# One cast and one subtraction for three split blocks, and another order in the last batch: a masked attention with a rational feed-forward layer

## The chip, the cores and the metric

The kernel runs on one core of a Trainium2 chip. A core has TensorE (PE, with weight loads listed apart as PEld), VectorE (DVE), ScalarE (ACT), GpSimd (POOL) and SyncE (SP), and DMA queues that SP, POOL and ACT issue into. The metric is the device time in microseconds (us) of one execution; the time before is the median of three runs. A separate profiled execution gives the trace.

## The reference

Inputs: q, k, v of 8 batches x 8 heads x 576 rows x 64; a number tau; w_in (512 x 2048), w_out (2048 x 512), and the coefficients a (4) and b (2).

```
scores = q @ k.T / 8
scores = where(scores >= max(scores) - tau, scores, -1e9)
attn   = softmax(scores)            # each row apart
x      = (attn @ v) laid out as 4608 tokens x 512
h      = x @ w_in
P      = a0 + a1 h + a2 h^2 + a3 h^3
Q      = 1 + |b0| |h| + |b1| h^2
out    = (P / (Q + 1e-6)) @ w_out
```

All inputs and the output are float32.

## The kernel before

**Attention units.** Two heads (a pair) are worked on at once; there are 4 pairs in a batch and 32 in all. The 576 rows of a pair make four full units of 128 rows and one short unit of 64 rows (number 4, the "rest"). A unit is: scores on TensorE into three PSUM banks (f_qk, L805 to L816), row maxima on VectorE (L822), threshold and mask on ScalarE (L829, L837), exponential with row sum on ScalarE (L841), reciprocal on VectorE (L852), the normalised weights split into a high and a low float16 half (L859 through the helper at L326 or L328, and L863), and two DMA transposes into a pT tile (L873). Two units of a pair share one pT tile (there are two), and then come three products with V on TensorE (f_av, L934), whose result is split into two float16 halves of x (L944, L950). The first batch takes another way through float32 transposes on TensorE (L886, L917).

**V.** V of a pair is loaded whole into one of NV tiles (L691, L695, L719), its largest magnitude is taken (L704 or L706), and when all four pairs of a batch have theirs, scale_ops (L412 to L445) makes one scale for the batch. After that each V is split into halves in place (L746 to L753, seen as L326, L328, L750, L320). A V tile is free again when the third product with it is done.

**Visits.** A batch is walked through in two visits of each pair: `half` (units 0 and 1), and later `other + rest` (units 2, 3 and the short one); the last pair takes all at once, and the second visits run backwards. K and Q are loaded at each visit (load_ops).

**Feed-forward chunks.** 256 tokens make a chunk: ("m", batch, 0) from units 0 and 1, ("m", batch, 1) from units 2 and 3, and the short rows of four batches make ("r", 0, 0) and ("r", 1, 0). Each chunk runs through four groups of four blocks of 128 hidden units (moe_ops). A group is: 48 float16 matmuls with w_in (L1051), the result to SBUF on ScalarE (L1060), the absolute value (L1065 or L1067), the rational function as a row of operations on 1024 columns (L1071 to L1093, of which L1078 and L1081 on ScalarE), and then the product with w_out. Of the four blocks, the first goes into that product as float32 (L1114); the other three (in_parts, PARTS = 3) are split into two parts of the type that TensorE multiplies faster: a cast (f_gh, seen as L318 on ScalarE or L320 on VectorE) and a subtraction (f_gl, L1101), each on 256 columns, into a g tile; then three matmuls for each half of the tokens (L1110). There are two g tiles. The last group of all is cut into two of two blocks. When a chunk's four groups are done, the sum is scaled (L1124, L1119) and stored (L1133 for an "m" chunk, one store a tile of 128 tokens; L1137 for an "r" chunk, two stores a tile).

**Weights.** w_in and w_out arrive as 64-bit numbers and are decoded on ScalarE and VectorE in the first part of the run, at times set by WHEN.

**Order.** Nothing is scheduled at run time. The program makes a list of operations, each with an engine (or two to choose from, FLEX) and a duration, a key, what it comes after and which buffers it takes (Hold) and drops. Plan.order walks through them in its own model of time: it starts on each engine the operation that can start first, and among those within TOL of it the one with the lowest key. Where two engines can do an operation, `sooner` weighs them with a price for each engine (START, EARLY and PRICE, by time). What comes out is one fixed order on each engine. Keys of attention units are their positions; a group of the feed-forward layer has the key max(previous + SPACING, last unit of its chunk + LEAD), those of the last batch end + ENDK + ENDS x i. LAST names the order of the last three chunks: ("m", 7, 0), ("m", 7, 1), ("r", 1, 0). A buffer that is not free holds up the engine that comes to the operation, and all behind it on that engine; so does a V load that waits on POOL's queue.

Of the kernel before, what the change touches and what calls it, by code (L numbers as in the profile page):

```python
# [8 lines left out]
F32 = mybir.dt.float32  # L9
F32R = mybir.dt.float32r  # L10
F16 = mybir.dt.float16
# [4 lines left out]
ALU = mybir.AluOpType  # L16
# [7 lines left out]

POOLS = {"e": 3, "hi": 2, "pT": 2, "st": 8, "sc": 2, "t": 8, "u": 3, "g": 2, "x": 3, "xr": 1}

B2, B3, BA, B1, BH = [(0, 1, 2), (3, 4, 5)], [(0, 1, 2)], [(3,), (4,), (5,)], [(7,), (6,), (5,)], [(5,), (6,)]


LEAD, SPACE0, SPACING = 4.776489494, 2.7365, 2.085146464
ENDK, ENDS = 4.7452, 10.130284218

WHEN = [(-4.7413, 1.6268), (5.5534, 0.8332), (13.0267, 0.2709), (15.0744, 0.5122)]

V0, V1 = -3.870384768, -4.680004432

SINGLE = 21

VISITED = 8

FIRST = [(0, 0, 8), (1, 0, 16), (0, 8, 16)]
LAST = (0, 1, 2)
SOON = 1

NQ = 2

NV = 5

EARLY_BP = 8

# [4 lines left out]
PARTS = 3  # L57
# [2 lines left out]

ALL = 2.0 ** 100

PLAIN = (0, 1, 2, 3, 4)

UP = 2.0 ** -14
TPD = 1.3
# [11 lines left out]
        "ev": {"ACT": 0.465, "DVE": 0.6}, "ev1": {"ACT": 0.156, "DVE": 0.196}, "A": {"ACT": 0.583, "DVE": 0.341},  # L78
        "gh": {"ACT": 0.31, "DVE": 0.2}, "wh": {"ACT": 0.57, "DVE": 0.38}, "vc": {"ACT": 0.7, "DVE": 0.25}, "twice": {"ACT": 0.2, "DVE": 0.13}}

START = {"ACT": 2.958800008, "DVE": 3.4788}
START_END = 61.53014116
EARLY = {"ACT": 2.0183, "DVE": 2.9268}
EARLY_END = 1205.239479456
PRICE = {"ACT": 0.7389, "DVE": 2.6699}

TOL = {"PE": 0.098890645, "ACT": 0.1137, "DVE": 0.0398, "POOL": 0.1, "DMA": 0, "GD": 0}
WARM, WARM_END = 0.6, 400.0

LOADS_END = 120.0  # L90

LATE = 2.0

SPARE = {'t': 2, 'u': 1, 'g': 1, 'sc': 1}

# [24 lines left out]
class Plan:  # L120
# [21 lines left out]
    def op(self, eng, dur, key, fn, after=(), take=(), drop=()):  # L142
        engs = {eng: dur} if isinstance(eng, str) else eng
        o = Op(engs, key, fn, [x for x in after if x is not None], list(take), list(drop))
        o.rank, o.tiling = self.rank, "ff"
        self.ops.append(o)
        return o
# [10 lines left out]
    def sooner(self, e, t, o, free, can):  # L158
        price = START if t < START_END else EARLY if t < EARLY_END else PRICE
        for x, dur in o.engs.items():  # L160
            if x != e:
                begin = max(free[x], o.ready[x])
                begin += sum(p.engs[x] for p in can[x] if p.key < o.key and len(p.engs) == 1 and p.ready[x] <= begin)
                if begin + dur * price[x] < t + o.engs[e] * price[e]:
                    return True
        return False

    def order(self):
# [6 lines left out]
        free = dict.fromkeys(engines, 0.0)  # L175
        tiling = "f"
# [13 lines left out]
        while left:  # L190
            best = None
            for e in engines:
                starts = []
                for o in can[e]:
                    t = max(free[e], o.ready[e])
                    for h in o.take:
                        spot = None if h.pool in line and line[h.pool][-1] is not h and len(self.pools.get(h.pool, ())) <= SPARE.get(h.pool, 99) else self.spot(h, t)
                        if spot is None:
                            t = None
                            break  # L200
                        t = max(t, spot[0])
                    if t is not None:
                        if e == "PE":
                            t = max(t, free[e] + TURN.get((tiling, o.tiling[0]), 0.0))
                        starts.append((t, o))
                if not starts:
                    continue
                first = min(t for t, _ in starts)
                starts = sorted([x for x in starts if x[0] <= first + TOL[e]] if all(len(o.engs) == 1 for _, o in starts)
                                else starts, key=lambda x: (x[1].key, x[1].n))  # L210

                keep = [(t, o) for t, o in starts if len(o.engs) == 1 or not self.sooner(e, t, o, free, can)]
                if not keep:
                    continue
                first = min(t for t, _ in keep)
                t, o = min(((t, o) for t, o in keep if t <= first + TOL[e]), key=lambda x: (x[1].key, x[1].n))
                if best is None or t < best[0]:
                    best = (t, o, e)
            assert best is not None, "no op can start"
            t, o, e = best  # L220
# [3 lines left out]
            if e == "PE" and self.warm is not None and t < WARM_END:  # L224
                n = int((t - free[e]) * WARM / 0.22)
# [10 lines left out]
            if e == "PE":  # L236
                tiling = o.tiling[1]
# [34 lines left out]
def fr(ap):  # L272
    return ap.bitcast(F32R)
# [3 lines left out]
def masked_attention_rational_ffn(  # L277
# [12 lines left out]
    nc = tc.nc  # L290
    B, NP, D, S = qT.shape
    S = S // 2
    DM, DFF = w_in.shape
    P = 128
    NT = S // P
    REM = S - NT * P
    NF = DFF // P
    NFP = NF // 2
    NC = DM // P
    CT = 256  # L300
# [4 lines left out]
    op = plan.op  # L305
# [10 lines left out]
    def copy(dst, src):  # L316
        if plan.eng == "ACT":
            nc.scalar.copy(dst, src)  # L318
        elif plan.eng == "DVE":
            nc.vector.tensor_copy(dst, src)  # L320
        else:
            nc.gpsimd.tensor_scalar(dst, src, 1.0, 1.0, ALU.mult, ALU.mult)
# [9 lines left out]
    def tensor_tensor(dst, x, y, how):  # L332
# [5 lines left out]

    forms = {"t": ([P, 4 * CT], F32), "u": ([P, DM], F32), "e": ([P, 2 * S], F32), "hi": ([P, 2 * S], F16),
             "pT": ([P, 2, 2, 2 * NT + 1, P], F16), "st": ([P, 8], F32), "sc": ([P, 4], F32),  # L340
             "g": ([P, 2, CT], F32), "x": ([P, 2, NP, CT], F16), "xr": ([P, 2, NP, CT], F16)}
    places = {x: [const.tile(f, d, name=f"{x}{i}") for i in range(POOLS[x])] for x, (f, d) in forms.items()}

    def place(h):
        return places[h.pool][h.slot]
# [181 lines left out]
    for i in range(NW):  # L527
        pieces = []
        for c in range(NC):
            n = i * NC + c  # L530
# [6 lines left out]
            key = w_key(i, c)  # L537

            o6, box = decode_ops(n, key, load, hold)
# [9 lines left out]
        key = w_key(i, NC)  # L549
# [17 lines left out]
    wo_done = []  # L567

    def in_parts(f):
        return f % NC >= NC - PARTS  # L570

    for f in range(NF):
# [6 lines left out]
        key = w_key(f // NC, NC + f % NC)  # L579
# [5 lines left out]
        o, box = decode_ops(NC * NW + f, key, load, hold)  # L585
# [15 lines left out]
    visits = []  # L601
    for bb in range(B):
        v0 = bb * NP
        if bb < VISITED:
            visits += [(v0 + i, half) for i in range(NP - 1)] + [(v0 + NP - 1, half + other + rest)]
            visits += [(v0 + i, other + rest) for i in range(NP - 2, -1, -1)]
        else:
            visits += [(v0 + i, half + other + rest) for i in range(NP)]
# [60 lines left out]

    def is_plain(bp, t):  # L670

        return bp < NP and t in PLAIN

    v_ops = {}

# [343 lines left out]
    def moe_ops(ck, f0, nb, p, begins, ends, soon):  # L1019
# [18 lines left out]
        def on(e, d, *rest):  # L1038
            return op(e, size(e, d), *rest)
# [52 lines left out]
        def f_g():  # L1092
            nc.vector.scalar_tensor_tensor(box["r"], box["r"], a0, box["q"], ALU.add, ALU.mult)  # L1093

        def f_gh(j):
            box["g", j] = place(hg[j])
            copy(fr(box["g", j][:, 0]), box["r"][:, j * CT:(j + 1) * CT])

        def f_gl(j):
            g = box["g", j]  # L1100
            nc.vector.tensor_tensor(fr(g[:, 1]), box["r"][:, j * CT:(j + 1) * CT], g[:, 0], ALU.subtract)  # L1101

        def f_g2(j, tt):
            f = f0 + j
            if begins and j == 0:
                acc[tt] = bank(ah[tt])
            if in_parts(f):
                g = box["g", j][:, :, tt * P:(tt + 1) * P]
                for n, (x, y) in enumerate(((0, 0), (1, 0), (0, 1))):
                    nc.tensor.matmul(acc[tt], fr(g[:, x]), fr(wo[f][y]), start=begins and j == n == 0,  # L1110
                                     stop=ends and j == nb - 1 and n == 2)
                return
            o = j * CT + tt * P
            nc.tensor.matmul(acc[tt], box["r"][:, o:o + P], wo[f], start=begins and j == 0, stop=ends and j == nb - 1)  # L1114
# [30 lines left out]
                                       wi_done[g] + x_done[ck] + wo_done[f0:f0 + nb] + last_g1 if prev is None else [prev],  # L1145
                                       [bhs[j // 2]] if (j % 2, part) == (0, 0) else (), [xo, xo])
        last_g1[:] = [prev]
        hh, hq, hr = Hold("t", 1), Hold("t", 1), Hold("t", 2 * nb)
        n = 1 if kind == "m" else 4
        hs = [b for b in ([bb] if kind == "m" else range(4 * bb, 4 * bb + 4))]  # L1150
        h = None
# [8 lines left out]
        r3 = on("DVE", 0.638, p + 0.67, f_r3, [r2])  # L1160
        ln = on("ACT", 0.632, p + 0.7, f_ln, [q, r3])
        iv = on("ACT", 0.563, p + 0.75, f_inv, [ln])
        e = on("DVE", 0.6075, p + 0.85, f_e, [iv])
        nn = on("DVE", 0.6075, p + 0.9, f_n, [e], (), [hh])
        gd = on("DVE", 0.638, p + 0.95, f_g, [nn, r3], (), [hq])
        hg, gl = {}, {}
        for j in range(nb):
            if in_parts(f0 + j):
                hg[j] = Hold("g", 2)
                o = op(FLEX["gh"], 0, p + 0.97, lambda j=j: f_gh(j), [gd], [hg[j]], [hr])  # L1170
                gl[j] = op("DVE", 0.335, p + 0.98, lambda j=j: f_gl(j), [o], (), [hr])
        if begins:
            accs[ck] = {}, [Hold("acc", 1, BA) for _ in range(2)]
        acc, ah = accs[ck]
# [3 lines left out]
            each.sort(key=lambda x: x[1])  # L1178
        for i, (j, tt) in enumerate(each):
            starts = begins and j == 0  # L1180
            o = op("PE", 0.705 if j in hg else 0.859, p + 1.7 + 0.1 * i, lambda j=j, tt=tt: f_g2(j, tt),
                   [gl.get(j, gd), wo_done[f0 + j], prev, None if starts else last_g2.get(tt)],
                   [ah[tt]] if starts else (), [hg.get(j, hr)])
            prev = last_g2[tt] = o
        if ends:
            prev = None
# [42 lines left out]
    for bb in range(1, B - 1):  # L1229
        order += [(("m", bb, c), range(0, NF, NC)) for c in range(2)]  # L1230
        if bb % 4 == 3:
            order.append((("r", bb // 4, 0), range(0, NF, NC)))
    p = 0.0
    for ck, fs in order:
        kind, bb, c = ck
# [61 lines left out]
```

## Time and profile before

| | us |
|---|---|
| median of three runs (lowest to highest) | 1279.27 (1278.4 to 1280.01) |
| the profiled execution's own time | 1281.68 |
| its span, from first to last instruction | 1279.9 |
| TensorE busy | 1246.4 (97%) |
| VectorE busy | 1199.3 (94%) |
| ScalarE busy | 1074.5 (84%) |
| GpSimd busy | 231.3 (18%) |

How to read the rows that the prediction shows. A row of the view by stretches gives the stretch, its length, and for each engine the time it was busy in it with the number of instructions; then the TensorE clock that was granted (1 is full), the busy share of the DMA engines and GB/s. A row of the waits gives who waited, for whom, the sum in us, how often, and the longest. A row of the groups gives line, engine, operation, result <- operands, shapes, count, then the sum of busy time and the mean duration in ns of one, then idle time of that engine just ahead of them and what ended it. A row of the timeline gives start, length (of all instructions merged into it), engine, line, operation and count. Matmul ends are modelled and matmuls overlap, so a busy TensorE isn't TensorE at its peak.

### The profile page before, as it was taken

To read this page: it belongs to the slowest core of one execution; us is meant where nothing else is said; L and a number is where in the kernel's file an instruction comes from. 1 tells how busy PE (TensorE), PEld (TensorE's weight loads), DVE (VectorE), ACT (ScalarE), POOL (GpSimd) and SP (SyncE) were. 2 spreads that over 40 slices of the span, in tenths; PEclk is the share of its full clock that TensorE was granted. 3 is DMA by queue.
4 is the path that set the end of the run, shared out by engine and by line. 5 is a ranking of instruction groups with operands and counts; after the bars stand their busy time and mean duration, and the time that the engine had idled before them with its cause. 6 is when DMAs were issued, how large, how long until landed. Compare 5 with 4: busy or idle time off the path is not lost.

```text
span 1279.9 us, 25127 instructions
## 1 busy us (share of the span) xinstructions
PE 1246.4 (97%) x9252; PEld 889.8 (70%) x9252; DVE 1199.3 (94%) x1960; ACT 1074.5 (84%) x2180; POOL 231.3 (18%) x480
## 2 busy tenths in 40 slices
PE   8899999999999999999999999999999999999998
PEld 6576676676767667766667667677776667677775
DVE  5899999999999999999999899999999999997876
ACT  5999888989999888888897699999988998874454
POOL 2112000132132311332022140322121221100000
PEclk9999999999999999999999999999999999999999
DMA  7645246688667656776442765876566665530000
GB/s 216 174 143 163 78 105 112 134 144 154 105 133 132 146 107 119 142 137 126 91 105 56 131 141 111 142 135 136 104 120 125 130 123 112 111 71 17 18 17 17
DMA packets 338251, 146.64 MB, mean 115 GB/s; under 512 B 314416, under 2 KB 320720, under 8 KB 338128
## 3 DMA queue, kind: packets, MB, share of 16 engines
q1 hardware_dynamic: 316528, 87.67, 38.5%
q0 software_dynamic: 21280, 56.78, 16.4%
q8 instruction: 73, 1.20, 0.4%
q10 hardware_dynamic: 320, 0.59, 0.2%
q14 instruction: 50, 0.41, 0.1%
HBM read 60.30 MB, written 9.44 MB: 54 GB/s over the span
## 4 chain that ended last, share of the span: by engine, by line
PE 53%; DVE 27%; ACT 8%; issue 5%; DMA 3%; SPq 0%; DVEq 0%; ACTq 0%
PE banks L1051 16%; PE banks L1110 15%; PE banks L1114 6%; PE banks L934 6%; PE banks L816 5%; DVE e L863 4%; DVE st L822 3%; DMA pT<-e 2%; DVE t L1071 2%; DVE t L1087 2%; DVE t L1090 2%; PE banks L805 2%; DVE t L1084 2%; DVE t L1093 2%; DVE g L1101 2%
## 5 line engine op out<-in xcount | busy, mean ns | idle before, releaser
L1051 PEld LDWEIGHTS <-wi 128*128 128x128 f16 x3456 | 324.1, 98 | 144.1 <-issue 108.0
L1051 PE MATMUL banks<-x,wi 128*128 128x256 f16 x3072 | 374.7, 275 | 3.0 <-ACT t L1060 1.7
L1110 PE MATMUL banks<-wp,g 128*128 128x512 f32 x1296 | 355.2, 415 | 1.9 <-ACT g L318 1.2
L1110 PEld LDWEIGHTS banks<-wp,g 128*128 128x128 f32 x1296 | 234.0, 189 | 70.9 <-issue 15.5
L837 ACT ACTIVATE e<-banks,st 128x576 f32<-128x576 f32 x288 | 206.4, 735 | 18.5 <-DVE st L831 11.1
L841 ACT ACTIVATE e<-e,cf 128x576 f32<-128x576 f32 x288 | 221.0, 774 | 0.3
L863 DVE SCALAR_TENSOR_TENSOR e<-e,st,hi 128x576 f16<-128x576 f32 x252 | 203.5, 808 | 3.9 <-ACT hi L326 3.4
L822 DVE TENSOR_REDUCE st<-banks 128x2 f32<-128x1152 f32 x128 | 171.8, 1342 | 12.9 <-PE banks L816 10.8
L326 ACT ACTIVATE hi<-e,st 128x576 f16<-128x576 f32 x177 | 134.0, 769 | 51.9 <-DVE st L852 41.1
L816 PE MATMUL banks<-KK,QQ 64*128 64x512 f32 x512 | 144.5, 641 | 0.0
L1114 PE MATMUL banks<-wp,t 128*128 128x512 f32 x288 | 142.2, 608 | 1.7 <-DVE t L1093 1.6
L1060 ACT ACTIVATE t<-banks,hsc 128x512 f32<-128x512 f32 (+1 forms) x192 | 106.3, 575 | 25.9 <-PE banks L1051 24.7
L934 PEld LDWEIGHTS <-V 128*64 128x64 f16 x2520 | 104.1, 111 | 33.8 <-issue 32.6
L934 PE MATMUL banks<-pT,V 128*64 128x256 f16 (+1 forms) x2520 | 118.9, 249 | 3.0 <-DMA pT<-e 3.0
L1087 DVE SCALAR_TENSOR_TENSOR t<-t,co,t 128x1024 f32<-128x1024 f32 (+1 forms) x73 | 92.0, 1261 | 22.7 <-ACT t L1081 22.7
L1078 ACT ACTIVATE t<-t,co 128x1024 f32<-128x1024 f32 (+1 forms) x73 | 82.7, 1133 | 12.8 <-DVE t L1084 12.7
L1093 DVE SCALAR_TENSOR_TENSOR t<-t,co,t 128x1024 f32<-128x1024 f32 (+1 forms) x73 | 92.0, 1261 | 0.5
L1071 DVE SCALAR_TENSOR_TENSOR t<-t,co 128x1024 f32<-128x1024 f32 (+1 forms) x73 | 92.0, 1260 | 0.0
L1084 DVE SCALAR_TENSOR_TENSOR t<-t,co,t 128x1024 f32<-128x1024 f32 (+1 forms) x73 | 91.9, 1260 | 0.0
L1074 DVE SCALAR_TENSOR_TENSOR t<-t,co 128x1024 f32<-128x1024 f32 (+1 forms) x73 | 91.9, 1259 | 0.0
L1101 DVE TENSOR_TENSOR g<-t,g 128x256 fp32r<-128x256 f32 x216 | 86.6, 414 | 2.0 <-ACT g L318 1.6
L1090 DVE SCALAR_TENSOR_TENSOR t<-t,t 128x1024 f32<-128x1024 f32 (+1 forms) x73 | 87.7, 1201 | 0.4
(137 smaller groups left out, 1518.2 us busy)
## 6 DMA issues: line engine op xcount, KB each, us to landing
KK<-in_kT_dram POOLq DMA_DIRECT2D x84, 144.0 KB, 3.9
t<-in_w_in_dram POOLq DMA_DIRECT2D x16, 512.0 KB, 5.8
t<-in_w_out_dram POOLq DMA_DIRECT2D x16, 512.0 KB, 4.7
V<-in_v_dram POOLq DMA_DIRECT2D x24, 256.0 KB, 4.4
out_dram<-u POOLq DMA_DIRECT2D x24, 256.0 KB, 2.7
QQ<-in_qT_dram POOLq DMA_DIRECT2D x42, 144.0 KB, 3.1
QQ<-in_qT_dram POOLq DMA_DIRECT2D x42, 128.0 KB, 3.4
KK<-in_kT_dram SPq DMA_DIRECT2D x24, 144.0 KB, 3.5
```

The costliest lines, as they stand in the source:

```text
L326: nc.scalar.activation(dst, src, AF.Identity, scale=factor)
L816: nc.tensor.matmul(d, QQ[r, t * P:(t + 1) * P], KK[r, REM:S], **one)
L822: nc.vector.tensor_reduce(box["st"][:, 0:2], box["both"], AX.X, ALU.max, negate=True)
L837: nc.scalar.activation(ev(hh), box["s"][hh], AF.Prelu, scale=SCALE, bias=box["st"][:, 2 + hh:3 + hh], alpha=STEEP)
L841: nc.scalar.activation(e, e, AF.Exp, scale=passes, accum_out=box["st"][:, 4 + hh:5 + hh])
L863: nc.vector.scalar_tensor_tensor(box["lo"][:, c], ev(hh), box["st"][:, 6 + hh:7 + hh], box["hi"][:, c], ALU.mult, ALU.subtract)
L934: nc.tensor.matmul(dst, V[:, c * P + head * D:c * P + (head + 1) * D], rhs, start=c == 0 and n == 0, stop=c == NT and n == 2)
L1051: nc.tensor.matmul(d, wi_tile(c, f0 + j, hl), x[:, c, :], start=c == 0 and n == 0, stop=c == NC - 1 and n == 2)
L1071: nc.vector.scalar_tensor_tensor(box["r"], box["h"], a2, box["h"], ALU.add, ALU.mult)
L1087: nc.vector.scalar_tensor_tensor(box["q"], box["q"], qc, box["i"], ALU.add, ALU.mult)
L1110: nc.tensor.matmul(acc[tt], fr(g[:, x]), fr(wo[f][y]), start=begins and j == n == 0, stop=ends and j == nb - 1 and n == 2)
L1114: nc.tensor.matmul(acc[tt], box["r"][:, o:o + P], wo[f], start=begins and j == 0, stop=ends and j == nb - 1)
```

## The change

The three split blocks of a group are cast by one instruction and subtracted by one, on 768 columns that lie side by side in the result, into one g tile three times as wide (one tile in place of two; one V tile less makes room). All split matmuls of the group come after that one subtraction, and the tile is free when the last of them is done. The cast is one operation, given to one engine as a whole (VectorE alone in the last group).

In the last batch the first visits take `half + rest`, the last pair takes everything, and the second visits take `other`. So the second "r" chunk is complete before the second "m" chunk. The first "m" chunk of that batch moves from the chunks after the end into those that are keyed among the attention units; after the end come ("r", 1, 0) and then ("m", 7, 1), which is now the last.

The constants of the planner change with it: LEAD, ENDK, ENDS, the fourth pair in WHEN, V0, the prices START and PRICE, EARLY_END (so that EARLY holds to the end) and TOL for VectorE. `sooner` also counts when the other engine's buffers come free. The dictionary PLAIN and STICK = 0.0 change nothing.

```
-POOLS = {..., "u": 3, "g": 2, "x": 3, "xr": 1}
+POOLS = {..., "u": 3, "g": 1, "x": 3, "xr": 1}
-LEAD, SPACE0, SPACING = 4.776489494, 2.7365, 2.085146464
-ENDK, ENDS = 4.7452, 10.130284218
-WHEN = [(-4.7413, 1.6268), (5.5534, 0.8332), (13.0267, 0.2709), (15.0744, 0.5122)]
-V0, V1 = -3.870384768, -4.680004432
+LEAD, SPACE0, SPACING = 4.46212747, 2.7365, 2.085146464
+ENDK, ENDS = 4.371514991, 7.461352888
+WHEN = [(-4.7413, 1.6268), (5.5534, 0.8332), (13.0267, 0.2709), (17.317172867, 0.340859863)]
+V0, V1 = -4.053118584, -4.680004432
-LAST = (0, 1, 2)
+LAST = (2, 1)
+REST_FIRST = (7,)
-NV = 5
+NV = 4
-START = {"ACT": 2.958800008, "DVE": 3.4788}
+START = {"ACT": 2.563365989, "DVE": 2.649650226}
-EARLY_END = 1205.239479456
-PRICE = {"ACT": 0.7389, "DVE": 2.6699}
+EARLY_END = 1317.950328776
+PRICE = {"ACT": 0.779887252, "DVE": 2.581335568}
-TOL = {..., "DVE": 0.0398, ...}
+TOL = {..., "DVE": 0.025166682, ...}
...
-                begin = max(free[x], o.ready[x])
+                begin = max([free[x], o.ready[x]] + [self.spot(h, 0.0)[0] for h in o.take])
...
-             "g": ([P, 2, CT], F32), ...
+             "g": ([P, 2, PARTS * CT], F32), ...
...
+        if bb in REST_FIRST:
+            visits += [(v0 + i, half + rest) for i in range(NP - 1)] + [(v0 + NP - 1, half + rest + other)]
+            visits += [(v0 + i, other) for i in range(NP - 2, -1, -1)]
...
-        def f_gh(j):
-            box["g", j] = place(hg[j])
-            copy(fr(box["g", j][:, 0]), box["r"][:, j * CT:(j + 1) * CT])
-        def f_gl(j):
-            g = box["g", j]
-            nc.vector.tensor_tensor(fr(g[:, 1]), box["r"][:, j * CT:(j + 1) * CT], g[:, 0], ALU.subtract)
+        split = [j for j in range(nb) if in_parts(f0 + j)]
+        GW = len(split) * CT
+        def f_gh():
+            box["g"] = place(hg)[:, :, 0:GW]
+            copy(fr(box["g"][:, 0]), box["r"][:, split[0] * CT:split[0] * CT + GW])
+        def f_gl():
+            g = box["g"]
+            nc.vector.tensor_tensor(fr(g[:, 1]), box["r"][:, split[0] * CT:split[0] * CT + GW], g[:, 0], ALU.subtract)
...
-        for j in range(nb):
-            if in_parts(f0 + j):
-                hg[j] = Hold("g", 2)
-                o = op(FLEX["gh"], 0, p + 0.97, lambda j=j: f_gh(j), [gd], [hg[j]], [hr])
-                gl[j] = op("DVE", 0.335, p + 0.98, lambda j=j: f_gl(j), [o], (), [hr])
+        n = len(split)
+        hg = Hold("g", 2 * n)
+        gh = {e: d * n + (n - 1) * -{"ACT": 0.098, "DVE": 0.07}[e] for e, d in FLEX["gh"].items() if e == "DVE" or not soon}
+        gh = op(gh, 0, p + 0.97, f_gh, [gd], [hg], [hr])
+        gl = op("DVE", 0.068 + 0.2667 * n, p + 0.98, f_gl, [gh], (), [hr])
...
+    order += [(x, range(0, NF, NC)) for i, x in enumerate((("m", B - 1, 0), ("m", B - 1, 1), ("r", B // 4 - 1, 0))) if i not in LAST]
```

More of the change, by code (lines that the diff above doesn't have):

```diff
@@ L23 @@
 TINY = 2.0 ** -60
-POOLS = {"e": 3, "hi": 2, "pT": 2, "st": 8, "sc": 2, "t": 8, "u": 3, "g": 2, "x": 3, "xr": 1}
+POOLS = {"e": 3, "hi": 2, "pT": 2, "st": 8, "sc": 2, "t": 8, "u": 3, "g": 1, "x": 3, "xr": 1}
 B2, B3, BA, B1, BH = [(0, 1, 2), (3, 4, 5)], [(0, 1, 2)], [(3,), (4,), (5,)], [(7,), (6,), (5,)], [(5,), (6,)]
-LEAD, SPACE0, SPACING = 4.776489494, 2.7365, 2.085146464
-ENDK, ENDS = 4.7452, 10.130284218
-WHEN = [(-4.7413, 1.6268), (5.5534, 0.8332), (13.0267, 0.2709), (15.0744, 0.5122)]
-V0, V1 = -3.870384768, -4.680004432
+LEAD, SPACE0, SPACING = 4.46212747, 2.7365, 2.085146464
+ENDK, ENDS = 4.371514991, 7.461352888
+WHEN = [(-4.7413, 1.6268), (5.5534, 0.8332), (13.0267, 0.2709), (17.317172867, 0.340859863)]
+V0, V1 = -4.053118584, -4.680004432
 SINGLE = 21
@@ L61 @@
 ALL = 2.0 ** 100
-PLAIN = (0, 1, 2, 3, 4)
+PLAIN = {0: (0, 1, 2, 3, 4), 1: (0, 1, 2, 3, 4), 2: (0, 1, 2, 3, 4), 3: (0, 1, 2, 3, 4)}
 UP = 2.0 ** -14
@@ L79 @@
         "gh": {"ACT": 0.31, "DVE": 0.2}, "wh": {"ACT": 0.57, "DVE": 0.38}, "vc": {"ACT": 0.7, "DVE": 0.25}, "twice": {"ACT": 0.2, "DVE": 0.13}}
-START = {"ACT": 2.958800008, "DVE": 3.4788}
+START = {"ACT": 2.563365989, "DVE": 2.649650226}
 START_END = 61.53014116
 EARLY = {"ACT": 2.0183, "DVE": 2.9268}
-EARLY_END = 1205.239479456
-PRICE = {"ACT": 0.7389, "DVE": 2.6699}
-TOL = {"PE": 0.098890645, "ACT": 0.1137, "DVE": 0.0398, "POOL": 0.1, "DMA": 0, "GD": 0}
+EARLY_END = 1317.950328776
+PRICE = {"ACT": 0.779887252, "DVE": 2.581335568}
+TOL = {"PE": 0.098890645, "ACT": 0.1137, "DVE": 0.025166682, "POOL": 0.1, "DMA": 0, "GD": 0}
 WARM, WARM_END = 0.6, 400.0
@@ L92 @@
 LATE = 2.0
+STICK = 0.0
 SPARE = {'t': 2, 'u': 1, 'g': 1, 'sc': 1}
@@ L215, in order @@
                 first = min(t for t, _ in keep)
-                t, o = min(((t, o) for t, o in keep if t <= first + TOL[e]), key=lambda x: (x[1].key, x[1].n))
+                near = [x for x in keep if x[0] <= first + TOL[e]]
+                t, o = min(near, key=lambda x: (x[1].key + (STICK if e == "PE" and x[1].tiling[0] != tiling else 0.0), x[1].n))
                 if best is None or t < best[0]:
@@ L340, in masked_attention_rational_ffn @@
              "pT": ([P, 2, 2, 2 * NT + 1, P], F16), "st": ([P, 8], F32), "sc": ([P, 4], F32),
-             "g": ([P, 2, CT], F32), "x": ([P, 2, NP, CT], F16), "xr": ([P, 2, NP, CT], F16)}
+             "g": ([P, 2, PARTS * CT], F32), "x": ([P, 2, NP, CT], F16), "xr": ([P, 2, NP, CT], F16)}
     places = {x: [const.tile(f, d, name=f"{x}{i}") for i in range(POOLS[x])] for x, (f, d) in forms.items()}
@@ L603, in masked_attention_rational_ffn @@
         v0 = bb * NP
-        if bb < VISITED:
+        if bb in REST_FIRST:
+            visits += [(v0 + i, half + rest) for i in range(NP - 1)] + [(v0 + NP - 1, half + rest + other)]
+            visits += [(v0 + i, other) for i in range(NP - 2, -1, -1)]
+        elif bb < VISITED:
             visits += [(v0 + i, half) for i in range(NP - 1)] + [(v0 + NP - 1, half + other + rest)]
@@ L670, in is_plain @@
     def is_plain(bp, t):
-        return bp < NP and t in PLAIN
+        return t in PLAIN.get(bp, ())
     v_ops = {}
@@ L1107, in f_g2 @@
             if in_parts(f):
-                g = box["g", j][:, :, tt * P:(tt + 1) * P]
+                o = (j - split[0]) * CT + tt * P
+                g = box["g"][:, :, o:o + P]
                 for n, (x, y) in enumerate(((0, 0), (1, 0), (0, 1))):
@@ L1147, in moe_ops @@
         last_g1[:] = [prev]
-        hh, hq, hr = Hold("t", 1), Hold("t", 1), Hold("t", 2 * nb)
+        hh, hq, hr = Hold("t", 1), Hold("t", 1), Hold("t", 2 * (nb - len(split) + 1))
         n = 1 if kind == "m" else 4
@@ L1162, in moe_ops @@
         iv = on("ACT", 0.563, p + 0.75, f_inv, [ln])
-        e = on("DVE", 0.6075, p + 0.85, f_e, [iv])
+        e = on("DVE", 0.638, p + 0.85, f_e, [iv])
         nn = on("DVE", 0.6075, p + 0.9, f_n, [e], (), [hh])
         gd = on("DVE", 0.638, p + 0.95, f_g, [nn, r3], (), [hq])
-        hg, gl = {}, {}
-        for j in range(nb):
-            if in_parts(f0 + j):
-                hg[j] = Hold("g", 2)
-                o = op(FLEX["gh"], 0, p + 0.97, lambda j=j: f_gh(j), [gd], [hg[j]], [hr])
-                gl[j] = op("DVE", 0.335, p + 0.98, lambda j=j: f_gl(j), [o], (), [hr])
+        n = len(split)
[3 more added lines that the diff above has]
+        gl = op("DVE", 0.068 + 0.2667 * n, p + 0.98, f_gl, [gh], (), [hr])
         if begins:
@@ L1180, in moe_ops @@
             starts = begins and j == 0
-            o = op("PE", 0.705 if j in hg else 0.859, p + 1.7 + 0.1 * i, lambda j=j, tt=tt: f_g2(j, tt),
-                   [gl.get(j, gd), wo_done[f0 + j], prev, None if starts else last_g2.get(tt)],
-                   [ah[tt]] if starts else (), [hg.get(j, hr)])
+            o = op("PE", 0.705 if j in split else 0.859, p + 1.7 + 0.1 * i, lambda j=j, tt=tt: f_g2(j, tt),
+                   [gl if j in split else gd, wo_done[f0 + j], prev, None if starts else last_g2.get(tt)],
+                   [ah[tt]] if starts else (), [hg if j in split else hr])
             prev = last_g2[tt] = o
```

## The prediction, made before the change was run

> **What bounds the kernel now.** I read the busy times by stretch first, since the change touches one stage in the middle and one at the end; then who TensorE waited for in the middle; then the groups of the cast and the subtraction; then the timeline at a batch boundary and at the end.
>
> ```profile
> core 0: us, PE busy (x) PEld busy (x) DVE busy (x) ACT busy (x) POOL busy (x), PEclk, DMA share, GB/s
> 0.00:120.00 120.00, 106.89 (x766) 78.82 (x766) 98.82 (x251) 103.98 (x226) 24.04 (x63) 0.99 0.58 169
> 120.00:1080.00 960.00, 945.64 (x7165) 667.35 (x7163) 933.68 (x1482) 851.67 (x1730) 200.21 (x404) 0.99 0.62 122
> 1080.00:1260.00 180.00, 180.00 (x1276) 135.19 (x1274) 155.13 (x210) 111.23 (x210) 7.09 (x14) 1.00 0.22 50
> 1260.00:1280.00 20.00, 13.86 (x53) 8.49 (x50) 11.65 (x20) 7.60 (x17) 0.00 (x0) 0.93 0.11 26
> 600.00:620.00 20.00, 17.68 (x124) 11.95 (x122) 17.51 (x23) 16.08 (x29) 1.22 (x3) 0.91 0.60 104
> 740.00:760.00 20.00, 17.79 (x140) 12.93 (x137) 18.41 (x36) 17.86 (x37) 7.37 (x15) 0.91 0.85 167
> ```
>
> From 120 to 1080 TensorE has work in flight for 945.64 of 960 us and VectorE for 933.68: two engines nearly full, with 14.4 and 26.3 us idle. From 1080 to 1260 TensorE has no gap at all, while VectorE has 24.9 us to spare. So VectorE time can be worth something only through those 14.4 us, through the first 120 us (13.1 us idle) and through the last 20 (6.1 us idle). No matmul is added or removed by the change, so the 1246 us that TensorE is busy stay nearly all. The two short stretches show that a gap costs more than itself: after 2.3 and 2.2 us of idle time the granted clock averaged 0.91, another 0.09 x 20 = 1.8 us each. The next rows say who caused the gaps of the middle (all but the smallest), and what VectorE's crowding does to ScalarE.
>
> ```profile
> PE banks L812 <- ACT e L837: 5.9, 5, 2.1
> PE banks L934 <- DMA pT<-e: 3.0, 2, 2.3
> PE banks L1051 <- ACT t L1060: 1.7, 2, 1.4
> PE banks L1110 <- ACT g L318: 1.2, 1, 1.2
> PE banks L1051 <- DVE xr L950: 1.2, 2, 0.9
> PE banks L1114 <- DVE t L1093: 0.4, 1, 0.4
> PE banks L1110 <- DVE g L1101: 0.4, 1, 0.4
> ...
> ACT hi L326 <- DVE st L852: 36.8, 43, 1.8
> ```
>
> TensorE waited 3.0 us for transposes and 10.8 for ScalarE or VectorE in these rows. ScalarE in turn waited 36.8 us for the small reciprocal (L852) that sits in VectorE's queue. A lighter VectorE queue shortens that chain.
>
> **The cast and the subtraction.**
>
> ```profile
> L1101 DVE TENSOR_TENSOR g<-t,g 128x256 fp32r<-128x256 f32 x216 | 86.6, 414 | 2.0 <-ACT g L318 1.6
> L318 ACT CAST g<-t 128x256 fp32r<-128x256 f32 x123 | 47.8, 401 | 41.9 <-PE banks L1110 35.7 <-DVE t L1093 5.3
> L320 DVE CAST g<-t 128x256 fp32r<-128x256 f32 x93 | 25.7, 285 | 2.2 <-PE banks L1110 1.5
> L592 DVE TENSOR_TENSOR wp<-t,wp 128x512 fp32r<-128x512 f32 x12 | 8.2, 683 | 0.1
> L320 DVE CAST wp<-t 128x512 fp32r<-128x512 f32 x8 | 3.5, 436 | 0.0
> L318 ACT CAST wp<-t 128x512 fp32r<-128x512 f32 x4 | 2.8, 688 | 0.3 <-DVE t L333 0.2
> ```
>
> 216 casts and 216 subtractions of 256 columns become 73 of each: 71 of 768 columns, one of 512, one of 256 (the last group of blocks is cut in two). The 768-column duration isn't in the trace; I extend the line through 256 and 512 columns. Subtraction: 683 + (683 - 414) = 952 ns; 71 x 0.952 + 0.683 + 0.414 = 68.7 us against 86.6, so VectorE gains 17.9. Cast: 587 ns on VectorE, 975 on ScalarE. With the engines shared as now (57% ScalarE, about 41 and 31 casts) ScalarE has 40 us in place of 47.8 and VectorE 18.2 in place of 25.7. VectorE's sum is then -25.4 and ScalarE's -7.8. The planner chooses the engine, so the ends are: all on VectorE, -17.9 + 16.7 = -1.2 for VectorE and -47 for ScalarE; all on ScalarE, -43.6 and +22. I take the present share, since both prices in the planner scale alike; either end still relieves one of the two.
>
> [...]
>
> 55 of the 73 blocks run in 120 to 1080, so some 19 of the 25.4 us fall there: VectorE's idle time grows from 26 to about 46 us. What TensorE waits there for the two engines is 10.8 us by the rows above; with nearly twice the slack I take half of it away, 5.4, and half of the two slow-clock losses, 1.8 of 3.6. Bounds: nothing (other orders make other gaps), and all of both, 14.4.
>
> The result is later, too: from the end of L1093 to the first split matmul it was a short cast and subtraction, 0.70 (VectorE) to 0.82 us, and becomes 1.54 to 1.93. What hides it is the unsplit block's matmuls, which need neither:
>
> ```profile
> 1237.81 1.28 DVE L1093 SCALAR_TENSOR_TENSOR t<-t,co,t 128x1024 f32<-128x1024 f32 x1
> 1239.71 1.88 PE L1114 MATMUL banks<-wp,t 128*128 128x512 f32 x4
> 1241.03 3.36 PE L1110 MATMUL banks<-wp,g 128*128 128x512 f32 x12
> 1244.82 1.64 PE L1110 MATMUL banks<-wp,g 128*128 128x512 f32 x6
> 1248.83 1.28 DVE L1093 SCALAR_TENSOR_TENSOR t<-t,co,t 128x1024 f32<-128x1024 f32 x1
> ```
>
> L1114 starts 0.6 us after L1093 ends and lasts about as long as the new pair, so I cost this at nothing; without that cover it is up to 0.3 us a group of blocks, 2.4 us over the last eight. The one large g tile also makes a cast wait until all 18 split matmuls of the group before are done. They end at 1246.5 here; the next L1093 ends at 1250.1. 3.6 us of slack, cost nothing. In return the wait for a free g buffer (35.7 us of ScalarE, most of it after 1120, where ScalarE is idle anyway) goes, and is worth nothing by itself.
>
> **Four V buffers in place of five.** Each batch holds four. Its scale needs the maximum of all four, so with four buffers the last V of a batch can be loaded only after the batch before has released its last one. At the boundary near 300 us:
>
> ```profile
> 294.26 0.73 ACT L706 ACTIVATE u<-V 128x640 bf16<-128x640 f32 x1
> 299.40 0.15 DVE L438 TENSOR_SCALAR isx<-sc 128x1 f32<-128x1 f32 x1
> 300.94 1.68 DVE L750 SCALAR_TENSOR_TENSOR V<-V,sx,u 128x640 f16<-128x640 f32 x2
> 301.44 1.83 PE L934 MATMUL banks<-pT,V 128*64 128x256 f16 x30
> 303.57 0.79 POOL L691 DMA_DIRECT2D V<-in_v_dram  x1 [3.37 <-PE banks L934]
> 318.94 1.83 PE L934 MATMUL banks<-pT,V 128*64 128x256 f16 x30
> ...
> V<-in_v_dram POOLq DMA_DIRECT2D x24, 256.0 KB, 4.4
> ```
>
> Now the load at 303.57 is the fifth and nobody hurries. After the change it is the fourth: 303.57 + 4.4 (landing) = 308.0; + 5.3 (294.26 to 299.55, maximum to scale) = 313.3; + 1.4 (to L750) + 0.9 (half of 1.68) + about 0.4 for the copy = 316.0. The attention product that needs it starts at 318.94 today. It fits with 2.9 us to spare, so zero, at seven boundaries; behind it in POOL's queue wait the next Q and K loads, which now stand behind the same release. The ends: nothing, and per boundary a stall like that of 600 to 620, 2.3 + 1.8 = 4.1 us, 28.7 for seven.
>
> **Last batch.** The short rows move into the first visit and the first chunk's four groups in among the attention units; the K loads' two extra 16 KB pieces on the queue move with them, none is added. TensorE's work in 1080 to 1260 is only reordered and it has no gap there: zero. After attention the chunk of short rows fills what the first chunk filled. Bounds: 2 us each way.
>
> **The end.**
>
> ```profile
> 1235.80 1.07 SPq L1133 DMA_DIRECT2D out_dram<-u  x2
> ...
> 1274.42 2.51 SPq L1137 DMA_DIRECT2D out_dram<-u  x4
> ```
>
> Short rows need two stores a tile, 256-token chunks one: one issue of 0.6 us less behind the last result. The last group's casts no longer wait for g buffers, 0.4 us. Together -1.0.
>
> **The start and the new constants** (engine prices, times of the fourth weight quarter, of V loads, LEAD) shift work within 0 to 120, where both helpers are near full: zero, with the 6.2 us that TensorE idles from 40 to 120 as bound either way.
>
> **Sum.** The profiled execution took 1281.68 us (span 1279.9 and 1.8 around it). -5.4 -1.8 -1.0 = -8.2 gives 1273.5. It lay 2.4 above the median of the three runs, 1279.27, so on that scale 1271.
>
> **Rivals.**
> Nothing comes of it: TensorE is the bound, its gaps come from the written-out order and others take their place. Only the end remains: 1278. For it: 945.64 of 960.
>
> VectorE is the real pacer: then its 19 us in the middle come off nearly whole, with 1.0 at the end: 1259. For it: 97% busy in 120 to 1080. Against: TensorE 98.5%. Inside it I see PEld at 667.35 of 960, 69.5%, and 75.1% (135.19 of 180) in the gapless end, as if the middle could be denser; but the mix differs, as attention matmuls stand only in the middle and early end. [...]
>
> Slower: the V chain misses at the boundaries. It decides when more than two of seven stall by 4.1 us, as that eats the 8.2. With four: 16.4 - 8.2 = 8.2 above today, 1287.5. For it: 2.9 us of margin against a wait from load to maximum of 9.2 us even where five were held (303.57 to the maximum at 312.79, row below). Against: two pT tiles let two more units go on, and feed-forward work is there to fill.
>
> ```profile
> 312.79 0.72 ACT L706 ACTIVATE u<-V 128x640 bf16<-128x640 f32 x1
> ```
>
> **How the numbers follow.** Forecast (5 to 13 us gained, so 1266 to 1275) 0.44; pacer (over 13) 0.14; nothing 0.22; V chain 0.20. 0.2% is 2.6 us, about what a measurement of this kernel can tell from no change. Faster: 0.44 + 0.14 + 0.05 of the third case; slower: the fourth and 0.01 of the third; same: the rest, 0.16. The range reaches to the pacer's 1259 and leaves out most of the V chain: 1259 to 1284.
>
> **What would show it.** Right: L1101 and its cast 73 each at about 952 and 590 or 975 ns; VectorE near 1174 us busy; TensorE's idle in the middle under 10 us; its waits for L837 and L1060 halved; one store last. Wrong: new gaps in front of L934 after a V load, of L1110 on g, or VectorE's freed time filled by casts and copies moved from ScalarE.

## The result, and the profile after

The changed kernel took 1272.5 us (median of five runs, 1268.9 to 1273.7) against 1279.7 for the kernel before: ratio 0.9941, 95% interval 0.9925 to 0.9957, 7.2 us less. The forecast was 1271. The profiled execution took 1270.73 us with a span of 1268.9. The busy times by stretch, cut at the same times as before (the same columns):

```profile
0.00:120.00 120.00, 106.89 (x776) 78.00 (x777) 103.93 (x256) 101.54 (x226) 25.48 (x66) 0.99 0.57 170
120.00:1080.00 960.00, 950.17 (x7292) 677.90 (x7291) 933.23 (x1326) 844.35 (x1682) 202.19 (x406) 1.00 0.62 122
1080.00:1260.00 180.00, 180.00 (x1185) 133.94 (x1183) 156.94 (x178) 107.74 (x187) 5.18 (x10) 1.00 0.22 48
1260.00:1280.00 20.00, 4.19 (x16) 2.53 (x14) 1.87 (x3) 1.37 (x2) 0.00 (x0) 0.90 0.07 26
```

TensorE got through 7292 matmuls from 120 to 1080 where it had done 7165; the gain was made there. Its idle time in that stretch went from 14.4 to 9.8 us and the granted clock from 0.99 to 1.00. In the first 120 us it idled 13.1 us as before, and from 1080 to 1260 it again had no gap. VectorE's row holds the surprise: 933.23 us busy from 120 to 1080 against 933.68 before, so it was no emptier than it had been.

The page's first part, then the groups of the merged instructions, and TensorE's waits from 120 to 1080:

```profile
PE 1241.3 (98%) x9262; PEld 892.4 (70%) x9262; DVE 1196.0 (94%) x1761; ACT 1055.0 (83%) x2094; POOL 232.8 (18%) x482
```

```profile
L1112 DVE TENSOR_TENSOR g<-t,g 128x768 fp32r<-128x768 f32 x71 | 67.3, 948 | 0.3
L323 ACT CAST g<-t 128x768 fp32r<-128x768 f32 x34 | 28.1, 825 | 6.5 <-DVE t L1101 4.8 <-PE banks L1122 1.7
L325 DVE CAST g<-t 128x768 fp32r<-128x768 f32 x37 | 20.5, 553 | 5.4 <-PE banks L1122 5.0
...
L333 DVE TENSOR_SCALAR hi<-e,st 128x576 f16<-128x576 f32 x83 | 42.2, 514 | 4.2 <-DMA pT<-hi 4.0
```

```profile
PE banks L820 <- ACT e L845: 5.7, 5, 3.1
PE banks L894 <- DVE u L887: 1.3, 1, 1.3
PE banks L820 <- ACT t L1136: 0.9, 1, 0.9
PE banks L1122 <- DVE g L1112: 0.8, 1, 0.8
PE banks L1059 <- ACT pT L323: 0.5, 1, 0.5
PE banks L942 <- DVE V L325: 0.2, 1, 0.2
```

(L820, L845, L942, L1059, L1112, L1122 are what L812, L837, L934, L1051, L1101, L1110 were.) The wait for transposes (3.0 us) and that of the first product for ScalarE's emptying of a bank (1.7) are gone; the largest, for L845, is as before (5.7 against 5.9). The cast and subtraction cost VectorE 22.7 us less (86.6 + 25.7 before; 67.3 + 0.7 + 0.4 and 20.5 + 0.4 + 0.3 now, the small ones from the two half groups), but VectorE as a whole is only 3.3 us less busy, and ScalarE 19.5 us less: the planner gave VectorE work that ScalarE had done, such as 8 more of the high halves (L333, 83 against 75).

### The profile page after: what moved, and what is told of

Its sections match the earlier page's. It is cut to its first block, busy times and chain, and to the rows that moved or that the text cites. A ratio compares the mean times of both kernels' runs of the same rounds, so it can differ in the third digit from the quotient of the medians.

```text
span 1268.9 us, 24830 instructions
## 1 busy us (share of the span) xinstructions
PE 1241.3 (98%) x9262; PEld 892.4 (70%) x9262; DVE 1196.0 (94%) x1761; ACT 1055.0 (83%) x2094; POOL 232.8 (18%) x482
## 4 chain that ended last, share of the span: by engine, by line
PE 71%; DVE 12%; ACT 3%; issue 3%; DMA 3%; POOL 1%; DVEq 0%; ACTq 0%; POOLq 0%
PE banks L1059 24%; PE banks L1122 20%; PE banks L1126 8%; PE banks L942 8%; PE banks L824 7%; PE banks L813 2%; PE banks L820 2%; DMA pT<-e 2%; DVE e L871 2%; DVE st L830 2%; DVE t L1079 1%; ACT e L845 1%; DVE t L1095 1%; DVE t L1092 1%; DVE t L1098 1%
## 5 line engine op out<-in xcount | busy, mean ns | idle before, releaser
L1059 PEld LDWEIGHTS <-wi 128*128 128x128 f16 x3456 | 325.8, 98 | 144.8 <-issue 109.7
L1059 PE MATMUL banks<-x,wi 128*128 128x256 f16 x3072 | 368.4, 273 | 0.5 <-ACT pT L323 0.5
L1122 PE MATMUL banks<-wp,g 128*128 128x512 f32 x1296 | 343.8, 410 | 1.6 <-DVE g L1112 1.1
L1122 PEld LDWEIGHTS banks<-wp,g 128*128 128x128 f32 x1296 | 235.2, 188 | 66.1 <-issue 11.2
L845 ACT ACTIVATE e<-banks,st 128x576 f32<-128x576 f32 x288 | 205.2, 735 | 13.6 <-DVE st L839 9.6
L331 ACT ACTIVATE hi<-e,st 128x576 f16<-128x576 f32 x169 | 128.9, 770 | 49.9 <-DVE st L860 46.6
L942 PEld LDWEIGHTS <-V 128*64 128x64 f16 x2520 | 104.0, 111 | 28.2 <-issue 25.1
L942 PE MATMUL banks<-pT,V 128*64 128x256 f16 (+1 forms) x2520 | 118.3, 248 | 0.3 <-DVE V L325 0.2
L1101 DVE SCALAR_TENSOR_TENSOR t<-t,co,t 128x1024 f32<-128x1024 f32 (+1 forms) x73 | 92.0, 1261 | 0.4
L1082 DVE SCALAR_TENSOR_TENSOR t<-t,co 128x1024 f32<-128x1024 f32 (+1 forms) x73 | 92.0, 1260 | 0.0
L1079 DVE SCALAR_TENSOR_TENSOR t<-t,co 128x1024 f32<-128x1024 f32 (+1 forms) x73 | 92.0, 1260 | 0.0
L1092 DVE SCALAR_TENSOR_TENSOR t<-t,co,t 128x1024 f32<-128x1024 f32 (+1 forms) x73 | 91.9, 1260 | 0.0
L655 POOL DMA_DIRECT2D QQ<-in_qT_dram x42 | 22.1, 527 | 345.0 <-PE banks L813 197.4
```

The source lines that it names most:

```text
L331: nc.scalar.activation(dst, src, AF.Identity, scale=factor)
L845: nc.scalar.activation(ev(hh), box["s"][hh], AF.Prelu, scale=SCALE, bias=box["st"][:, 2 + hh:3 + hh], alpha=STEEP)
L942: nc.tensor.matmul(dst, V[:, c * P + head * D:c * P + (head + 1) * D], rhs, start=c == 0 and n == 0, stop=c == NT and n == 2)
L1059: nc.tensor.matmul(d, wi_tile(c, f0 + j, hl), x[:, c, :], start=c == 0 and n == 0, stop=c == NC - 1 and n == 2)
L1079: nc.vector.scalar_tensor_tensor(box["r"], box["h"], a2, box["h"], ALU.add, ALU.mult)
```

## The experiments

Three theories were put on record. Slack: lighter VectorE and ScalarE queues let TensorE wait less. Order: the gain is only another written-out order, with its constants and last batch. Pacer: VectorE's busy time comes off the run nearly whole. The first three kernels keep the changed kernel's order on every engine and alter only what one operation issues.

**Three of 256 columns, same order.**

```
-            copy(fr(box["g"][:, 0]), box["r"][:, split[0] * CT:split[0] * CT + GW])
+            for i, j in enumerate(split):
+                copy(fr(box["g"][:, 0, i * CT:(i + 1) * CT]), box["r"][:, j * CT:(j + 1) * CT])
   (and the subtraction likewise)
```

> The changed kernel with its order of work on every engine kept as it is, but each wide cast and subtraction issued as three of 256 columns. So the planner's part of the change (order, last batch, constants, buffers) stays, and only the time of the instructions goes back: VectorE gets about 18 us more for subtractions (216 x 0.40 against 67.3 + 1.1) and about 10 for its casts, ScalarE about 12 for its casts. Slack theory (the gain comes from lighter VectorE and ScalarE queues, so that TensorE waits less): the gain goes, 1272.5 + 5 to 8 = 1277 to 1281. Order theory (the gain is the other order with its new constants and last batch; TensorE is the bound): within 2.6 us of the changed kernel, 1270 to 1275. Pacer theory (VectorE sets the pace): + 20 or more, above 1290.

1279.5 us, ratio to before 0.9996 (0.9983 to 1.0009): the whole gain is gone, 7.0 us. The doses were about half of those expected, 13.7 us more for VectorE and 5.8 for ScalarE, as three instructions in a row overlap (216 subtractions of 424 ns each, 91.6 us in sum, keep VectorE busy for 78.8). Both engines got more, and the order had been written for the merged durations, so the 7.0 us are what the merged instructions are worth in this order, and not VectorE's share alone.

**One more subtraction of 256 columns, same order.**

```
+            nc.vector.tensor_tensor(fr(g[:, 1, 0:CT]), box["r"][:, split[0] * CT:(split[0] + 1) * CT], g[:, 0, 0:CT], ALU.subtract)
```

> The changed kernel in the same order, with one more subtraction of 256 columns in each group, written over what is there already: VectorE alone gets 73 x 0.35 to 0.42 = 25 to 30 us more, 20 to 23 of it between 120 and 1080 us, where it idles 26.8. Slack theory: the slope of the prediction, 7.2 us for 25.4 us of VectorE, gives + 7 to 8: about 1280. Order theory: within 2.6 us, 1270 to 1275. Pacer theory: + 20 and more, above 1292.

1297.2 us, ratio 1.0134 (1.0116 to 1.0153): 24.7 us over the changed kernel, more than the slack theory allows and what the pacer theory asked for.

**The first polynomial step on half of its columns, same order** (the other half of that step is left out).

```
-            nc.vector.scalar_tensor_tensor(box["r"], box["h"], a2, box["h"], ALU.add, ALU.mult)
+            W = FW // 2
+            nc.vector.scalar_tensor_tensor(box["r"][:, 0:W], box["h"][:, 0:W], a2, box["h"][:, 0:W], ALU.add, ALU.mult)
```

> The changed kernel in the same order, with the first operation of the rational function (L1079, 1024 columns) done on half of its columns only, so a part of the polynomial is left out. VectorE gets 73 x 0.53 = 39 us of slack more, and nothing else changes. Slack theory: TensorE idles 9.8 us between 120 and 1080, of which some 8 by waits for ScalarE and VectorE; half of it or more goes: 4 to 8 us faster, 1265 to 1269. Order theory: nothing, 1270 to 1275. Pacer theory: most of 39 us, below 1245.

1268.8 us, ratio 0.9908 (0.9888 to 0.9927): 3.7 us under the changed kernel for 29.8 us less of VectorE. The dose was smaller than the 39 expected. The gain is a little less than the slack theory's 4 to 8, and refutes the pacer in this direction.

The first parts of the pages of these three (half the columns, three of 256, one more), then each one's row of 120 to 1080:

```profile
PE 1241.7 (98%) x9262; PEld 894.3 (71%) x9262; DVE 1166.2 (92%) x1761; ACT 1056.5 (83%) x2094; POOL 233.0 (18%) x482
```

```profile
PE 1248.6 (98%) x9262; PEld 894.2 (70%) x9262; DVE 1209.7 (95%) x1979; ACT 1060.8 (83%) x2162; POOL 234.5 (18%) x482
```

```profile
PE 1257.0 (97%) x9262; PEld 893.3 (69%) x9262; DVE 1226.4 (95%) x1834; ACT 1055.3 (81%) x2094; POOL 233.4 (18%) x482
```

```profile
120.00:1080.00 960.00, 951.02 (x7302) 679.76 (x7301) 912.91 (x1332) 848.16 (x1686) 203.10 (x406) 1.00 0.63 122
```

```profile
120.00:1080.00 960.00, 946.36 (x7188) 670.18 (x7186) 933.93 (x1486) 838.73 (x1710) 202.37 (x404) 1.00 0.63 121
```

```profile
120.00:1080.00 960.00, 941.38 (x7117) 662.25 (x7116) 933.87 (x1354) 824.51 (x1645) 201.05 (x404) 0.99 0.61 120
```

| VectorE busy, whole run | median | us of run per us of VectorE, against the changed kernel |
|---|---|---|
| 1166.2 (half) | 1268.8 | 3.7 / 29.8 = 0.12 |
| 1196.0 (changed) | 1272.5 | |
| 1209.7 (three of 256; ScalarE + 5.8) | 1279.5 | 7.0 / 13.7 = 0.51 |
| 1226.4 (one more) | 1297.2 | 24.7 / 30.4 = 0.81 |

It is a bend, not a line. In the stretch, VectorE is busy for some 933 of 960 us in all but the first: I read that as filled as far as this order lets it be, as what is added makes the stretch do less (7292, 7188, 7117 matmuls). With half the columns VectorE idles 47 us there, and TensorE gets through hardly more than in the changed kernel (7302). The loss doesn't all show as idle time of TensorE: the same 9262 matmuls keep it busy for 1241.3 us in the changed kernel, 1248.6 with three of 256 and 1257.0 with one more. How VectorE holds up ScalarE, and that TensorE, shows in two waits over the whole run, of half the columns, of the changed kernel, of three of 256, and of one more:

```profile
ACT hi L331 <- DVE st L860: 31.3, 53, 1.3
...
PEld banks L820 <- ACT e L845: 11.6, 16, 4.1
```

```profile
ACT hi L331 <- DVE st L860: 46.6, 59, 1.6
...
PEld banks L820 <- ACT e L845: 11.4, 19, 3.4
```

```profile
ACT hi L331 <- DVE st L860: 53.5, 64, 2.1
...
PEld banks L820 <- ACT e L845: 20.8, 36, 3.8
```

```profile
ACT hi L331 <- DVE st L860: 64.3, 70, 2.3
...
PEld banks L820 <- ACT e L845: 26.9, 46, 4.5
...
PEld banks L1123 <- DVE g L1113: 10.4, 19, 2.5
```

The more VectorE has to do, the longer ScalarE waits for the small reciprocal; with more than in the changed kernel TensorE finds the score banks not yet read 36 and 46 times in place of 19. With half the columns ScalarE waits 15 us less, and TensorE no less (11.6 against 11.4): this is the bend once more. That one wait makes the other fits these rows, and no run takes them apart. The last row is the added subtraction standing directly in front of TensorE, so up to 10 us of the 24.7 can be this chain's and not the queue's.

**A repetition.**

> The kernel before with one constant moved by a trifle: LEAD 4.786489494 in place of 4.776489494 (a hundredth of an attention unit later for every feed-forward group). No work is added or removed; only the written-out order can change. Slack theory: within 2.6 us of before, 1277 to 1282. Order theory: a different order by itself moves the time by several us, either way, as the kernel before is one draw out of many: 1273 or 1287 would be as good.

1278.5 us, 0.9985 (0.9967 to 1.0003). The instructions came out in the same order on all five engines, so this says nothing on orders: it is the kernel before once more, and shows that a repetition agrees within 0.2%.

The next four take the change apart, and here the planner writes a new order each time.

**The merging alone** (old constants, old last batch, one wide g tile, four V tiles).

> The kernel before with the wide cast and subtraction alone (one wide g tile and so four V tiles), with its old constants and its old last batch; the planner writes a new order for the new durations. Three instructions in place of one cost 7.0 us in the changed kernel's order, so if the merging is all of the gain: 1270 to 1275. If the gain needs the constants that came with it: 1276 to 1282. If four V tiles cost something that the constants make up for: above 1282.

1281.7 us, 1.0008 (0.9994 to 1.0022). No gain.

**The new constants alone.**

```
-LEAD, ... = 4.776489494     +LEAD, ... = 4.46212747      (and ENDK, ENDS, WHEN, V0, START, PRICE, EARLY_END, TOL, sooner)
```

> The kernel before with the new constants alone (and the buffer test in the choice of engine): three casts and subtractions, five V tiles, two g tiles, old last batch. Merging as the cause: within 4 us of before, 1276 to 1284, as a new order with no time saved. Constants as the cause: 1270 to 1275.

1309.7 us, 1.0241 (1.0208 to 1.0274): 30 us slower than before. Neither theory had it.

**New constants and new last batch without the merging.**

> The changed kernel without the merging: new constants and new last batch, but three casts and subtractions that the planner knows of, two g tiles and five V tiles. Merging as the cause: 1275 to 1283 (the end alone gives 1.0 us). Order, constants and last batch as the cause: 1270 to 1275. Against the order that was planned for the merged instructions and got three each (1279.5), it shows whether it is the planning or the instructions.

1313.6 us, 1.0266 (1.0234 to 1.0299). In the changed kernel's order the same three instructions took 1279.5, so 34 us lie in the order that is written when the planner knows of them.

**The changed kernel with the old last batch.**

```
-LAST = (2, 1)      +LAST = (0, 1, 2)
-REST_FIRST = (7,)  +REST_FIRST = ()
```

> The changed kernel with the old last batch (short rows last in the second visit, chunks in the order first, second, short rows, all after the end). Prediction: only the end changes, one store issue and the shorter wait, + 1.0: 1273 to 1275. If the last batch's rearrangement carries the gain (TensorE lost 4 us less between 960 and 1080): 1276 to 1280.

1274.5 us, 0.9962 (0.9947 to 0.9978): 2.0 us slower than the changed kernel, with overlapping intervals. The last batch carries a small part at most, and the intervals don't settle how much. The 4 us of the expectation aren't in TensorE's idle time from 960 to 1080, which went from 1.57 us before to 0.01 in the changed kernel.

The rows of 120 to 1080 of the merging alone and of the constants alone, and the latter's waits of TensorE there:

```profile
120.00:1080.00 960.00, 946.47 (x7195) 673.27 (x7195) 927.75 (x1314) 845.66 (x1681) 202.42 (x406) 1.00 0.64 122
```

```profile
120.00:1080.00 960.00, 928.01 (x7016) 652.87 (x7015) 915.82 (x1454) 836.34 (x1693) 199.28 (x401) 0.99 0.62 120
```

```profile
PE banks L1051 <- ACT t L1060: 11.7, 9, 3.8
PE banks L812 <- ACT e L837: 9.7, 8, 3.3
PE banks L1114 <- DVE t L1093: 3.4, 3, 1.8
```

With the merging alone VectorE idles 32 us where it idled 26, and TensorE 13.5 where it idled 14.4: some slack came and was hardly used. With the constants alone TensorE and VectorE idle more at once, 32 and 44 us, in an order in which TensorE waits 11.7 us for L1060, against 1.7.

So the last four try how much an order by itself decides. Each has one constant moved a little and does the same work as its parent; in all four the order differs from the parent's.

**SPACING 2.080 in place of 2.085 in the kernel before.**

> The kernel before with SPACING 2.080146464 in place of 2.085146464: no work is added or removed, and this time the written-out order does differ from before (the first try, LEAD by a hundredth, came out as the same order on all engines). Draw theory (the time depends on which order the planner happens to write, as before and the constants alone lie 30 us apart): several us off, to the slower side if the constants of before were a good draw, 1282 to 1310. Merging theory: within 4 us of before, 1276 to 1284.

1283.4 us, 1.0031 (1.0016 to 1.0046).

**LEAD a hundredth up in the constants-only kernel.**

> The constants-only kernel (1309.7) with LEAD 4.47212747 in place of 4.46212747, which writes another order. If 1309.7 was one bad draw, this one lies nearer to before: 1279 to 1300. If these constants don't suit a kernel without the merging at all, it stays above 1300.

1295.6 us, 1.0125 (1.0099 to 1.0151).

**LEAD a hundredth up in the merged-only kernel.**

> The merged-only kernel (1281.7) with LEAD 4.786489494 in place of 4.776489494, another order. Merging theory: the merging is worth up to 7 us, and a mean over draws would lie below before: 1272 to 1279. If the merging alone is worth nothing whatever the order: 1278 to 1286.

1290.3 us, 1.0093 (1.0060 to 1.0126).

**LEAD a hundredth up in the changed kernel.**

> The changed kernel with LEAD 4.47212747 in place of 4.46212747, another order. If its 1272.5 is the merging's worth with any order: 1268 to 1277. If it is a picked draw among orders that scatter by several us: slower, 1277 to 1295.

1277.0 us, 0.9982 (0.9965 to 0.9999).

| | three instructions | merged |
|---|---|---|
| old constants | 1279.7 and 1283.4 | 1281.7 and 1290.3 |
| new constants | 1309.7 and 1295.6 | 1272.5 and 1277.0 |

(The new constants stand with the old last batch in the left column and with the new one in the right; with the new one the left has 1313.6, with the old one the right has 1274.5.)

A trifle in one constant moved the time by 4 to 14 us, from half of what the change did to twice that. Of the merged pairs only the one with the new constants lies below before, and of the unmerged pairs none does. The second order of the changed kernel keeps only some 2 us of the gain (ratio 0.9982), so most of the 7.2 hangs on the one order. That the merging needs these constants, and they the merging, holds in both draws of each; how far a mean over many orders would show it, two draws can't say. The merged instructions in the order of the kernel before were not run.

## Why the prediction was right, and where it wasn't

**The gain in the middle, 5.4 + 1.8 = 7.2 us: its size held, its reason in part.** In the changed kernel's order the merged instructions are worth 7.0 us. TensorE's idle time there fell by 4.5 us, to 9.8. But of the two waits that were to be halved, that for L845 stayed at 5.7, and that of the first product (1.7) went whole; the transposes' wait (3.0), which I had kept, went too. "A lighter VectorE queue shortens that chain" was not what happened, as the queue got no lighter: ScalarE's wait for the reciprocal from 120 to 1080 grew from 36.8 to 44.9 us.

```profile
ACT hi L331 <- DVE st L860: 44.9, 57, 1.6
```

The clock gave more than I had put down. Before, three stretches of 20 us in the middle were at 0.91: the two that I had counted, and 140 to 160. After, one was. First two rows of before, then the one of after:

```profile
140.00:160.00 20.00, 19.83 (x114) 14.22 (x115) 18.99 (x51) 15.47 (x35) 1.06 (x2) 0.91 0.35 109
...
700.00:720.00 20.00, 17.16 (x161) 11.24 (x161) 15.06 (x25) 11.97 (x26) 4.20 (x10) 1.00 0.74 106
```

```profile
700.00:720.00 20.00, 16.91 (x130) 11.45 (x128) 13.75 (x23) 11.26 (x24) 2.06 (x7) 0.91 0.78 104
```

At my price of 0.09 x 20 = 1.8 us a stretch that is an estimate of 3.6 us gained, not 1.8. It fits that TensorE's busy time, which I had as staying, fell from 1246.4 to 1241.3 us. Nor does the idle time of a stretch alone decide its clock: from 700 to 720 the kernel before idled 2.8 us at a clock of 1.00, from 140 to 160 only 0.2 us at 0.91. So the 1.8 us that a gap was to cost beyond itself stay an estimate, which no run shows by itself.

Taken as something that merging gives by itself, the step fell: merged alone gave 1281.7 and 1290.3.

**VectorE near 1174 us: wrong, 1196.0.** The casts and subtractions gave up 22.7 us (25.4 predicted), and the planner refilled the queue; it was ScalarE that got lighter. I had listed this refilling as what would show me wrong. The subtraction was 948 ns (952 predicted) and VectorE's cast 553 (587). ScalarE's cast was 825, not 975: the 512-column row I extended from, 688 ns, was four casts in the decoding of the weights and not on one line with 401 and 825, which has 613 at 512 columns.

**The new constants at zero, bound 6.2 us: wrong in size.** They made 30.0 us in the kernel without merging, to the slower side, and 16 in its second order. I had looked at which stretch they move work into, and not at the whole order that follows from each of them. So the forecast's number is in good part luck: it had no term for the order, and it came out because order and instruction times happened to fit. The "nothing" rival named this mechanism, and the merged-only kernel is that rival.

**Four V buffers at zero: right, though the sum was not.** The same boundary after the change:

```profile
303.07 0.79 POOL L699 DMA_DIRECT2D V<-in_v_dram  x1 [1.91 <-PE banks L942]
...
312.01 0.73 ACT L714 ACTIVATE u<-V 128x640 bf16<-128x640 f32 x1
...
317.37 0.15 DVE L443 TENSOR_SCALAR isx<-sc 128x1 f32<-128x1 f32 x1
318.95 1.67 DVE L758 SCALAR_TENSOR_TENSOR V<-V,sx,u 128x640 f16<-128x640 f32 x2
...
321.15 1.83 PE L942 MATMUL banks<-pT,V 128*64 128x256 f16 x30 [0.23 <-DVE V L325]
```

From load to maximum it took 8.9 us, not 4.4: nobody hurried here either. The last copy of V (L325) released the product only at 321.15, where the sum had V ready by 316.0; the margin of 2.9 us was more than used up. It cost TensorE 0.23 us, since it had feed-forward and score matmuls to go on with, and no other boundary shows such a wait in TensorE's rows of 120 to 1080. That, and not the margin, is the cover.

**One wide g tile and the later result at zero: right.** TensorE idled 0.8 us for L1112 in the middle; ScalarE's wait for a free g buffer went from 35.7 to 1.7 us, and no run shows by itself what that was worth. The 0.3 us a group that the prediction sets as the price without cover isn't worked out in it; by its own durations the result is up to 1.93 less 0.82, 1.1 us, later.

**The end, 1.0 us: near.** The last ScalarE instruction was followed by 4.1 us before (1275.80 to 1279.9) and by 3.2 after; its row before, then the last store and its row after:

```profile
1275.11 0.69 ACT L1124 ACTIVATE u<-banks,co 128x512 f32<-128x512 f32 x1 [0.71 <-PE banks L1110]
```

```profile
1264.28 1.74 SPq L1145 DMA_DIRECT2D out_dram<-u  x2
1264.97 0.69 ACT L1136 ACTIVATE u<-banks,co 128x512 f32<-128x512 f32 x1 [0.72 <-PE banks L1122]
```

1264.97 + 0.69 = 1265.66, and 3.2 to 1268.9: 0.9 us from the end, where 1.0 was put down. With the old last batch 2.0 us came back, which the intervals can't tell from 1.0.

**The pacer rival** was right about one side only: added VectorE time costs up to 0.81, VectorE time saved in the same order gives 0.12. The row by weight-load time that spoke for it (69.5%) stood at 70.6% after (677.90 of 960) and 70.8% with VectorE relieved by 29.8 us (679.76), so VectorE isn't what keeps it under the end's; that the mix of matmuls does is argued, not shown.

## What to carry to other kernels

Where two engines are both nearly full, cost a saving on the second engine twice, at a fixed order and with the order written anew: the first tells what the instructions are worth in that order (here 7.0 us), the second may give it all away. Before crediting a change to its mechanism, move one constant by a trifle and see that the order really differs, so as to know the scatter that orders bring (4 to 14 us here). Constants picked for one set of durations are part of the kernel: with three instructions in place of one they cost 16 to 34 us.

## What was not expected of the hardware

Three subtractions of 256 columns in a row cost VectorE less than their 424 ns each: 78.8 us for 216, 365 ns a piece, as they overlap, where between other instructions they had cost 401 (86.6 us for 216). The wide one at 948 ns saves 0.15 us a group against a row of three and 0.26 against scattered ones.

```profile
L1114 DVE TENSOR_TENSOR g<-t,g 128x256 fp32r<-128x256 f32 x216 | 78.8, 424 | 0.0
```
